# Gated linear attention, then a squared-ReLU feed-forward: the first four chunks loaded as two pairs, zero products in PE's early row, new figures for the plan

## The chip, the cores and the metric

One core of a Trainium2 chip runs the whole program. The metric is device time in microseconds of one execution; the lower, the better. The engines are PE (TensorE, matrix products), DVE (VectorE), ACT (ScalarE), POOL (GpSimd) and SP (SyncE, which issues the transfers here).

## The reference

```python
def _attn_ref(q, k, v, alpha):            # each (4, 8, 768, 48): batch, heads, tokens, width
    state = np.zeros((B, H, D, D))
    for t in range(S):
        state = alpha[:, :, t, :, None] * state + np.einsum('bhd,bhe->bhde', k[:, :, t], v[:, :, t])
        y[:, :, t] = np.einsum('bhd,bhde->bhe', q[:, :, t], state)
    return y

def _moe_ref(x, w_in, w_out):             # x: (3072, 384), w_in: (384, 2048), w_out: (2048, 384)
    r = np.maximum(x @ w_in, 0.0)
    return (r * r) @ w_out
```

The output of the first, transposed to one row of 384 per token, is the input of the second. All inputs and the output are float32.

## The kernel before

The 3072 tokens are 24 chunks of 128, six for each batch. A chunk lies with one token per partition. Its recurrence is done in closed form:

- `ln`: ACT takes the logarithm of alpha. `pm`: PE sums it over the tokens with a triangular matrix (and with a column of ones for the decay of the whole chunk). `ainv`, `am`: ACT takes exp(-sum) and exp(sum).
- `km`: POOL multiplies k by ainv. `qm`: DVE multiplies q by am. `vc`: POOL casts v to bf16.
- `tr`, `qkT`: PE transposes both, DVE copies them out of PSUM. (From chunk `N_PE` = 14 on a DMA transposes instead.) `sc`: PE forms the scores, 8 products. `sm`: DVE masks them with the triangle.
- `av`: PE multiplies the scores with v and adds q times the state of the chunks before (`sb`). `st`, `dec`, `sb`: the state gets the chunk's part, DVE decays it, ACT casts it.
- `xn`, `px`, `xT`: the result is cast, transposed by PE and copied into `xT`, the input of the feed-forward part.

The feed-forward part works on nine groups of 2 or 3 chunks. For each of 16 slices of 128 of the inner width, `mm1` is three products into `ph` (L393), `relu` is ACT's (L398, tile `r`) and `sq` is DVE's square (L404, tile `gT`). `m2` then multiplies `gT` with the second weights into `po` (L427); the result is copied to `ob` and stored.

A class `Plan` sets the order of everything. Each step is added with an engine, a cost, a key (its due time) and the steps that it needs; `Plan.run` plays the program through with these costs, and the instructions are emitted in the order of that play. Each engine then executes its own row strictly in that order, and waits in it on semaphores. `HOP` is what the play adds from a step's end to its use by another engine, `QUEUE` how far SP may run ahead of its transfers. PSUM has one bank set for `pm` and `py` together (`m`), one for `sc`, one for the transposes (`t`), two for `ph` and one for `po`.

SP issues all transfers, in one queue: alpha, k, q and v of chunks 0 to 3, then four loads of the first weights, chunk 4, four loads of the second weights, and the other chunks. A load of one chunk (`load_chunk`, L353) is 128 partitions x 8 heads x 48 floats, 1024 rows of 192 B, as each head's tokens lie apart in memory. A load of the first weights (L368) is 128 x 3 rows of 2 KB. The weights land in four buffers `wst`, and POOL casts them to bf16 (L372).

Of the kernel before, what the change touches and what calls it, by code (L numbers as in the profile page):

```python
# [14 lines left out]
class Plan:  # L15
# [3 lines left out]
    HOP = {"PE": 0.28, "SP": 0.0}  # L19
    QUEUE = 4.0  # L20
# [5 lines left out]
    def add(self, eng, cost, key, emit, after=(), behind=(), acquire=None,  # L26
            release=None, load=None):
        op = dict(eng=eng, cost=cost, key=(key, len(self.ops)), emit=emit,
                  after=[o for o in after if o is not None],
                  behind=[o for o in behind if o is not None], acquire=acquire,  # L30
                  release=release, load=load, start=None, done=None)
        self.ops.append(op)
        return op

    def run(self):
        ops, cap = self.ops, self.cap
        waiting = {id(o): 0 for o in ops}
# [10 lines left out]
        now = 0.0  # L48
        order = []
        while len(order) < len(ops):  # L50
            for r in [f for f in frees if f[0] <= now]:
                frees.remove(r)
                cap[r[1]] += 1
            chosen = None
            for t, o in ready:
                if t > now or free[o["eng"]] > now:
                    continue
                if o["acquire"] and cap[o["acquire"]] < 1:
                    continue
                if chosen is None or o["key"] < chosen["key"]:  # L60
                    chosen = o
            if chosen is None:
                later = [max(t, free[o["eng"]]) for t, o in ready] + [f[0] for f in frees]
                now = min(x for x in later if x > now)
                continue
            o = chosen
            ready = [x for x in ready if x[1] is not o]
            o["start"] = now
            free[o["eng"]] = now + o["cost"]
            if o["load"]:  # L70
                bus = max(bus, now + o["cost"]) + o["load"]
# [20 lines left out]
def kernel(  # L92
# [13 lines left out]
    P = 128  # L106
# [8 lines left out]
    NW = 4  # L115
    N_PE = 14
# [4 lines left out]
    ar = alpha.rearrange("b h (c p) d -> b c p h d", p=P)  # L121
    w_in_r = moe_w_in.rearrange("(j p) f -> p j f", p=P)
# [6 lines left out]
    wst = ctx.enter_context(tc.tile_pool(name="wst", bufs=4))  # L129
# [27 lines left out]
    qks = [consts.tile([P, 2, H, DP], BF16, name=f"qk{i}") for i in range(NS)]  # L157
    sbs = [consts.tile([P, NP, 2 * D], BF16, name=f"sb{i}") for i in range(2)]
    xTs = [consts.tile([P, KT, len(cs) * P], BF16, name=f"xT{g}") for g, cs in enumerate(groups)]

    def setup():
        nc.vector.memset(utri, 1.0)
        nc.gpsimd.affine_select(
            out=utri, in_=utri, compare_op=ALU.is_ge, fill=0.0,
            base=0, pattern=[[0, 1], [1, P]], channel_multiplier=-1,
        )
        nc.vector.memset(ones_col, 1.0)
        nc.vector.memset(lns[0], 0.0)
        make_identity(nc, ident)
        for x in lns[1:] + qks[:2]:  # L170
            nc.vector.memset(x, 0.0)
        for x in qks[2:] + sbs:
            nc.gpsimd.memset(x, 0.0)
# [11 lines left out]
    def o(kind, n):  # L185
        return O.get((kind, n))

    def gla(n):
# [100 lines left out]
        def e_xn():  # L289
            T["xn", n] = work.tile([P, HD], BF16, name="xn")  # L290
            nc.scalar.copy(T["xn", n], T["py", n][:, 0:HD])  # L291

        def e_px():
            px = T["px", n] = ps_t.tile([P, KT, P], BF16, name="px", tag="t")
            for j in range(KT):
                nc.tensor.transpose(px[:, j, :], T["xn", n][:, j * P:(j + 1) * P], ident)  # L296

        def e_xT():
            g = group_of[n]
            col = groups[g].index(n) * P  # L300
            nc.vector.tensor_copy(xTs[g][:, :, col:col + P], T["px", n])

# [5 lines left out]
        def e_qd():  # L308
# [5 lines left out]
        add("ln", "ACT", 0.53, e_ln, [o("ld_a", n), o("pm", n - NS)])  # L314
        add("vc", "POOL", 0.62, e_vc, [o("ld_v", n), o("av", m), o("st", m)])
        add("pm", "PE", 0.27, e_pm, [o("ln", n), o("av", n - NW + 1)], acquire="m")
        add("ainv", "ACT", 0.49, e_ainv, [o("pm", n), o("km", m)])
        add("am", "ACT", 0.49, e_am,
            [o("pm", n), o("qm", m), o("ainv", n), o("dec", m)], release="m")
        add("km", "POOL", 0.92, e_km, [o("ainv", n), o("ld_k", n), o("st", n - NS), o("tr", n - NS)])  # L320
        add("qm", "DVE", 0.80, e_qm, [o("am", n), o("ld_q", n), o("tr", n - NS)])
        if n < N_PE:
            add("tr", "PE", 0.45, e_tr, [o("km", n), o("qm", n)], acquire="t")
            add("qkT", "DVE", 0.69, e_qkT, [o("tr", n), o("av", m), o("sc", m)], release="t")
# [4 lines left out]
        add("sc", "PE", 0.40, e_sc, [o("qkT", n)], acquire="sc")  # L329
        add("sm", "DVE", 1.22, e_sm, [o("sc", n), o("av", m)], release="sc")  # L330
        add("av", "PE", 0.25 if first else 0.42, e_av,
            [o("sm", n), o("vc", n)] + ([] if first else [o("sb", n - 1)]), acquire="m")
        add("xn", "ACT", 0.48, e_xn, [o("av", n), o("px", m)], release="m")
# [5 lines left out]
        if n < N_PE:  # L339
            add("px", "PE", 0.18, e_px, [o("xn", n)], acquire="t")  # L340
            add("xT", "DVE", 0.36, e_xT, [o("px", n)], release="t")
        else:
            O["xT", n] = O["px", n] = plan.add("SP", 0.6, -2e6 + n, e_xd, [o("xn", n)], load=0.7)

    loaded = []

    def load_chunk(n):
        b, c = divmod(n, NCH)
        last_use = {"a": "ln", "k": "km", "q": "qm", "v": "vc"}
        for name, src in (("a", ar), ("k", kr), ("q", qr), ("v", vr)):  # L350
            def emit(name=name, src=src):
# [4 lines left out]
                [o(last_use[name], n - NLD)], loaded[-1:], load=1.03)  # L356
            loaded.append(O["ld_" + name, n])

    weights = []

    def load_w(kind, i):
# [8 lines left out]
        def cast():  # L370
# [10 lines left out]
    def moe(g):  # L381
# [7 lines left out]
        def unit1(f):  # L389
# [6 lines left out]
            def e_relu():  # L396
                r = T["r", g, f] = rp.tile([P, 4 * P], BF16, name="r")
                nc.scalar.activation(r[:, 0:tg], T["ph", g, f][:, 0:tg], AF.Relu)  # L398

            def e_sq():  # L400
                if f == 0:
                    T["gT", g] = gp.tile([P, FT, 4 * P], BF16, name="gT")
                r = T["r", g, f]
                nc.vector.tensor_mul(T["gT", g][:, f, 0:tg], r[:, 0:tg], r[:, 0:tg])  # L404
            u = g * FT + f
# [4 lines left out]
                [o("xT", n) for n in cs] + [O["cwi", f // 4]], [prev], acquire="ph")  # L410
# [3 lines left out]
            free = [O.get(("m2", n, 3)) for n in groups[g - 2]] if g >= 2 else []  # L414
            O["sq", u] = plan.add("DVE", 0.12 + 0.34 * part, key - 3 * PACE, e_sq,
                                  [rl] + free, [O.get(("sq", u - 1))])

        def unit2(tt, n, qd):
            bank = "m" if g >= len(groups) - 2 and n % 2 else "po"

            def e_mm():
                if qd == 0 and bank == "po":
                    T["po", n] = ps_o.tile([P, d_model], FP32, name="po")
# [11 lines left out]
            if qd == 3:  # L435
# [9 lines left out]
                def e_out():  # L445
                    nc.sync.dma_start(out=out_r[n], in_=T["ob", n])
# [55 lines left out]
```

## Time and profile before

| | |
|---|---|
| median of 3 runs | 198.18 us (197.69 to 198.73) |
| the profiled execution | 198.69 us |
| span of its instructions | 196.7 us |
| PE busy | 174.7 us, 89% of the span |
| DVE, ACT, POOL busy | 130.2, 119.7, 50.0 us |
| DMA | 33.77 MB, 121749 packets, 115072 of them under 512 B |

The page gives busy times over the whole span and in 40 slices of 4.9 us. The slices are digits of tenths; the row PEclk has the granted clock of PE. A row of the timeline has start, duration, engine, line, operation, tiles, count, and in brackets the idle time before it with what ended it. "idle" of a group is the idle time of its engine just before it.

### The profile page before, as it was taken

The numbers are of one execution on the slowest core, as the hardware profiler recorded it, in microseconds if no ns is written. First come the engines' busy times: TensorE is split into PE (matmuls) and PEld (weight loads), VectorE is DVE, ScalarE is ACT, GpSimd is POOL, SyncE is SP. The second block draws the span as 40 slices with busy tenths as digits, with TensorE's granted clock in tenths as the row PEclk, the third lists the DMA queues.
The fourth block names the chain that finished last, engine by engine and source line by source line (L and its number), as shares of the span: only waits on it lengthen the run. The fifth ranks groups of instructions, "written<-read, shape, count | busy, mean of one in ns | idle before, by whom it ended". The sixth has DMA issues, their size and how long they took to land.

```text
span 196.7 us, 4408 instructions
## 1 busy us (share of the span) xinstructions
PE 174.7 (89%) x1618; PEld 115.0 (58%) x1618; DVE 130.2 (66%) x260; ACT 119.7 (61%) x293; POOL 50.0 (25%) x67
## 2 busy tenths in 40 slices
PE   0466698599999999999999999998999999999992
PEld 0355475366666666766664666565565666567761
DVE  4366677996488889888956785594686763445311
ACT  3354259437536998788866777665776755465400
POOL 6242464660434233331420321111221000000000
PEclk9999999969999999999999999999999999999999
DMA  6999999999989999898999998999985422111012
GB/s 121 187 188 202 355 308 264 382 214 197 191 174 244 185 202 187 153 223 156 227 140 222 224 206 127 194 200 169 190 186 125 106 72 60 40 41 44 36 44 80
DMA packets 121749, 33.77 MB, mean 172 GB/s; under 512 B 115072, under 2 KB 120192, under 8 KB 121728
## 3 DMA queue, kind: packets, MB, share of 16 engines
q1 hardware_dynamic: 121728, 33.50, 85.3%
q8 instruction: 12, 0.20, 0.5%
q14 instruction: 9, 0.07, 0.1%
HBM read 25.17 MB, written 4.72 MB: 152 GB/s over the span
## 4 chain that ended last, share of the span: by engine, by line
PE 68%; DVE 9%; DMA 7%; SPq 6%; ACT 4%; issue 3%; POOL 1%; ACTq 0%; POOLq 0%
PE ph L393 26%; PE po L427 24%; SPq L353 5%; DMA ld_v<-in_v_dram 5%; DVE gT L404 4%; PE pom L427 4%; PE sc L246 3%; PE pt L234 3%; DMA ld_a<-in_alpha_dram 3%; PE py L265 2%; PE py L260 2%; ACT r L398 2%; PE st L274 1%; PE px L296 1%; PE pm L208 1%
## 5 line engine op out<-in xcount | busy, mean ns | idle before, releaser
L398 ACT ACTIVATE r<-ph 128x384 bf16<-128x384 f32 (+1 forms) x144 | 63.8, 455 | 34.6 <-PE ph L393 33.3
L393 PE MATMUL ph<-xT,w_in_b 128*128 128x384 bf16 (+1 forms) x432 | 81.6, 315 | 2.3 <-ACT r L398 1.5
L404 DVE TENSOR_TENSOR gT<-r 128x384 bf16<-128x384 bf16 (+1 forms) x144 | 56.4, 406 | 35.1 <-ACT r L398 32.9
L427 PE MATMUL po<-w_out_b,gT 128*128 128x384 bf16 x336 | 66.5, 328 | 0.5 <-ACT ob L441 0.4
L393 PEld LDWEIGHTS <-w_in_b 128*128 128x128 bf16 x432 | 40.1, 99 | 23.8 <-issue 5.1
L427 PEld LDWEIGHTS <-gT 128*128 128x128 bf16 x384 | 36.0, 98 | 22.1 <-issue 1.3
L225 POOL TENSOR_TENSOR qk<-ld_k,ainv 128x384 bf16<-128x384 f32 x24 | 22.0, 919 | 53.0 <-ACT ainv L217 53.0
L251 DVE TENSOR_TENSOR sm<-sc,utri 128x1024 bf16<-128x1024 f32 x24 | 29.3, 1221 | 4.0 <-PE sc L246 3.8
L204 POOL CAST vb<-ld_v 128x384 bf16<-128x384 f32 x24 | 13.2, 551 | 40.7 <-DMA ld_v<-in_v_dram 33.5
L228 DVE TENSOR_TENSOR qk<-ld_q,am 128x384 bf16<-128x384 f32 x24 | 17.8, 740 | 7.6 <-ACT am L222 7.5
L200 ACT ACTIVATE ln<-ld_a 128x384 bf16<-128x384 f32 x24 | 12.7, 528 | 9.5 <-DMA ld_a<-in_alpha_dram 9.3
L291 ACT CAST xn<-py 128x384 bf16<-128x384 f32 x24 | 11.5, 478 | 8.6 <-PE py L265 8.6
L217 ACT ACTIVATE ainv<-pm 128x384 bf16<-128x384 f32 x24 | 11.7, 489 | 6.3 <-PE pm L212 5.8
L265 PE MATMUL py<-vb,sm 128*128 128x48 bf16 x192 | 12.2, 190 | 3.7 <-DVE sm L251 2.5
L208 PE MATMUL pm<-ln,utri 128*128 128x384 bf16 x24 | 8.4, 352 | 6.5 <-ACT ln L200 5.6
L265 PEld LDWEIGHTS <-sm 128*128 128x128 bf16 x192 | 10.4, 101 | 6.0 <-DVE sm L251 4.5
L282 DVE TENSOR_TENSOR st<-st,am 128x384 f32<-128x384 f32 x20 | 11.2, 561 | 3.3 <-PE st L274 3.1
L234 PE MATMUL pt<-ident,qk 128*128 128x128 bf16 x112 | 10.5, 246 | 2.7 <-POOL qk L225 1.6
L222 ACT ACTIVATE am<-pm 128x388 f32<-128x388 f32 (+1 forms) x24 | 11.9, 495 | 0.0
L246 PE MATMUL sc<-qkT 64*128 64x128 bf16 x192 | 10.6, 236 | 1.0 <-DVE qkT L238 1.0
L441 ACT COPY ob<-po 128x384 f32<-128x384 f32 x12 | 5.8, 482 | 8.5 <-PE po L427 8.4
L260 PE MATMUL py<-sb,qkT 128*128 128x96 bf16 x80 | 10.8, 212 | 0.0
(34 smaller groups left out, 118.2 us busy)
## 6 DMA issues: line engine op xcount, KB each, us to landing
ld_a<-in_alpha_dram SPq DMA_DIRECT2D x24, 192.0 KB, 4.3
ld_k<-in_k_dram SPq DMA_DIRECT2D x24, 192.0 KB, 4.4
ld_q<-in_q_dram SPq DMA_DIRECT2D x24, 192.0 KB, 4.4
ld_v<-in_v_dram SPq DMA_DIRECT2D x24, 192.0 KB, 4.3
out_dram<-ob SPq DMA_DIRECT2D x24, 192.0 KB, 2.5
wst<-in_moe_w_in_dram SPq DMA_DIRECT2D x4, 768.0 KB, 8.5
wst<-in_moe_w_out_dram SPq DMA_DIRECT2D x4, 768.0 KB, 7.4
qkT<-qk SPq DMA_TRANSPOSE x10, 3.7
```

The costliest lines, as they stand in the source:

```text
L204: nc.gpsimd.tensor_copy(T["vb", n], T["v", n])
L225: nc.gpsimd.tensor_mul(qk[:, 1, :, 0:D], heads(T["k", n]), heads(T["ainv", n]))
L228: nc.vector.tensor_mul(qk[:, 0, :, 0:D], heads(T["q", n]), heads(T["am", n][:, 0:HD]))
L234: nc.tensor.transpose(pt[:, w, p, :], qk[:, w, 2 * p:2 * p + 2, :], ident)
L246: nc.tensor.matmul(sc[:, i, p, :], lhsT=qkT[r, 1, p, :], rhs=qkT[r, 0, p, :], start=True, stop=True)
L251: nc.vector.tensor_mul(sm.rearrange("s i p t -> s (i p) t"), T["sc", n].rearrange("s i p t -> s (i p) t"), utri.to_broadcast([P, H, P]))
L260: nc.tensor.matmul(py[:, 2 * p * D:2 * (p + 1) * D], lhsT=qkT[:, 0, p, :], rhs=sb[:, p, :], start=True, stop=False, skip_group_check=True)
L265: nc.tensor.matmul(py[:, h * D:(h + 1) * D], lhsT=sm[:, i, p, :], rhs=vb[:, h * D:(h + 1) * D], start=first, stop=True, skip_group_check=True)
L393: nc.tensor.matmul(ph[:, 0:tg], lhsT=w_in_b[:, j, f * P:(f + 1) * P], rhs=xT[:, j, 0:tg], start=(j == 0), stop=(j == KT - 1))
L398: nc.scalar.activation(r[:, 0:tg], T["ph", g, f][:, 0:tg], AF.Relu)
L404: nc.vector.tensor_mul(T["gT", g][:, f, 0:tg], r[:, 0:tg], r[:, 0:tg])
L427: nc.tensor.matmul(T["po", n], lhsT=T["gT", g][:, kf, tt * P:(tt + 1) * P], rhs=w_out_b[:, kf, :], start=(kf == 0), stop=(kf == FT - 1))
```

## The change

**Loads.** Chunks 0 and 1, and 2 and 3, are loaded as pairs: one transfer for alpha, one for k, q and v each, in which a partition gets two tokens that follow each other, so that a row is 2 x 48 floats, 384 B, and a transfer has 1024 of them. The pairs lie in the buffers `wst`, of which there are now six; alpha and k share one, q and v another. The even tokens of a pair form one slot and the odd ones the other (`j`), and what was chunk 0 and chunk 1 is now the lower and the upper half of the partitions (`x`).

**Recurrence of the pairs.** `gla_pair` takes both slots through `ln`, `pm`, `ainv`, `am`, `km`, `qm`, `vc`, `tr` and `qkT`, then both through `sc` and `sm`, then both halves through `av` and the rest. `pm` has two products for the sums instead of one, `sc` 16 instead of 8 (of 64 rows of output), `av` two for each head instead of one, `st` 8 instead of 4. `qkT` of the second slot is a copy on ACT. Masks for the four combinations of slots are built in `setup`. The output of these chunks is stored in two transfers each.

**Zero products.** Steps `blank`, each one product of a 128 x 128 zero tile with 256 zero columns into the `po` bank, fill PE's row wherever the play finds PE idle, up to the first `m2`. There are 117 of them in the program: 20 ahead of the first `pm`, 99 ahead of the first `mm1`.

**Figures.** `HOP` of PE goes from 0.28 to 0.17, `QUEUE` from 4.0 to 3.0, and many costs change. The play now charges DVE and POOL for one another where both use SBUF (`port`), and PE's products at up to double cost until 6.2 us after the first dense one.

```diff
-    HOP = {"PE": 0.28, "SP": 0.0}
-    QUEUE = 4.0
+    HOP = {"PE": 0.17, "SP": 0.0}
+    QUEUE = 3.0
...
+            if o["eng"] == "PE":
+                if o["dense"] and warm is None:
+                    warm = now + 6.2
+                if warm is None or now < warm:
+                    o["cost"] *= 2.0 if o["dense"] else 1.5
+            if o["port"]:
+                other = "DVE" if o["eng"] == "POOL" else "POOL"
+                o["cost"] += max(0.0, held[other] - now)
+                held[o["eng"]] = now + o["cost"]
...
+    NWST = 6
+    PAIRS = (0, 1)
+    NBLANK = 300
...
+    qr2, kr2, vr2, ar2 = [x.rearrange("b h (s p j) d -> b s p h (j d)", p=P, j=2)
+                          for x in (q, k, v, alpha)]
-    wst = ctx.enter_context(tc.tile_pool(name="wst", bufs=4))
+    wst = ctx.enter_context(tc.tile_pool(name="wst", bufs=NWST))
...
-        for x in qks[2:] + sbs:
+        for x in [blank] + qks[2:] + sbs:
             nc.gpsimd.memset(x, 0.0)
...
+        def e_pm(n, j):
+            pm = T["pm", n] = ps_m.tile([P, HD + 2 * NP], FP32, name="pm2", tag="m")
+            l0, l1 = lns[n0 % NS], lns[(n0 + 1) % NS]
+            nc.tensor.matmul(pm[:, 0:HD], lhsT=uinc2, rhs=l0[:, :, 0:D], start=True, stop=False)
+            nc.tensor.matmul(pm[:, 0:HD], lhsT=uinc2 if j else ustr2, rhs=l1[:, :, 0:D],
+                             start=False, stop=True)
...
+    def load_pair(S):
+        b, c = divmod(S, NCH // 2)
+        for name, src in (("a", ar2), ("k", kr2), ("q", qr2), ("v", vr2)):
+            def emit(name=name, src=src):
+                if name in "aq":
+                    T["w2", S, name in "qv"] = wst.tile([P, 2, H, 2, D], FP32, name="pair", tag="wst")
+                x = T[name + "2", S] = T["w2", S, name in "qv"][:, int(name in "kv")]
+                nc.sync.dma_start(out=x.rearrange("p h j d -> p h (j d)"), in_=src[b, c])
...
-        add("pm", "PE", 0.27, e_pm, [o("ln", n), o("av", n - NW + 1)], acquire="m")
+        add("pm", "PE", 0.29, e_pm, [o("ln", n), o("av", n - NW + 1)], acquire="m")
-        add("qm", "DVE", 0.80, e_qm, [o("am", n), o("ld_q", n), o("tr", n - NS)])
+        add("qm", "DVE", 0.55, e_qm, [o("am", n), o("ld_q", n), o("tr", n - NS)], port=True)
...
+    def e_blank():
+        if "blank" not in T:
+            T["blank"] = ps_o.tile([P, 4 * P], FP32, name="po")
+        nc.tensor.matmul(T["blank"][:, 0:2 * P], lhsT=blank[:, 0:P], rhs=blank,
+                         start=True, stop=True)
+    for i in range(NBLANK):
+        plan.add("PE", 0.107, 1e6 + i, e_blank, dense=True, drop=O["m2", 0, 0])
```

Where it moves instructions, at three places. First SP's row up to the weights; `ld_a` to `ld_v` are the loads of one chunk, `pair` the new ones. Before, from chunk 2 on:

```order
L353 DMA ld_a_163<-in_alpha_dram 128x8x48
L353 DMA ld_k_169<-in_k_dram 128x8x48
L353 DMA ld_q_182<-in_q_dram 128x8x48
L353 DMA ld_v_187<-in_v_dram 128x8x48
L353 DMA ld_a_208<-in_alpha_dram 128x8x48
L353 DMA ld_k_213<-in_k_dram 128x8x48
L353 DMA ld_q_234<-in_q_dram 128x8x48
L353 DMA ld_v_251<-in_v_dram 128x8x48
L368 DMA wst_275<-in_moe_w_in_dram 128x3x512
```

Now, from the start:

```order
L567 DMA pair_158<-in_alpha_dram 128x8x96
L567 DMA pair_158<-in_k_dram 128x8x96
L567 DMA pair_167<-in_q_dram 128x8x96
L567 DMA pair_167<-in_v_dram 128x8x96
L567 DMA pair_179<-in_alpha_dram 128x8x96
L567 DMA pair_179<-in_k_dram 128x8x96
L567 DMA pair_204<-in_q_dram 128x8x96
L567 DMA pair_204<-in_v_dram 128x8x96
L598 DMA wst_254<-in_moe_w_in_dram 128x3x512
```

The first weights stand behind eight transfers instead of sixteen, with the same bytes.

Second, PE's row at its beginning. Before, it opens with the sums of chunk 0, and nothing stands ahead of them:

```order
L208 LDWEIGHTS utri
L208 MATMUL pm<-ln_100,utri 128x384
L212 LDWEIGHTS ln_100
L212 MATMUL pm<-ones_col,ln_100 128x1
...
L234 LDWEIGHTS qk_104
L234 MATMUL pt<-ident,qk_104 128x128
```

Now the last of the 20 zero products, the sums of the first slot, and the first of seven zero products ahead of the sums of the second:

```order
L716 LDWEIGHTS blank
L716 MATMUL po<-blank 128x256
L263 LDWEIGHTS uinc_110
L263 MATMUL pm_189<-ln_100,uinc_110 128x384
L264 LDWEIGHTS ustr_111
L264 MATMUL pm_189<-ln_101,ustr_111 128x384
L716 LDWEIGHTS blank
```

`pm` of the first slot now needs both slots' `ln`, and stands behind products that need nothing but the cleared tile.

Third, DVE's row up to the first squares (`gT`). Before, chunks 1 to 3 follow each other:

```order
L251 TENSOR_TENSOR sm<-sc,utri 128x1024
L228 TENSOR_TENSOR qk_106<-ld_q,am 128x8x48
L282 TENSOR_TENSOR st<-st,am 128x384
L238 COPY qkT<-pt 128x1024
L301 COPY xT_110<-px 128x3x128
L251 TENSOR_TENSOR sm<-sc,utri 128x1024
L228 TENSOR_TENSOR qk_107<-ld_q,am 128x8x48
L282 TENSOR_TENSOR st<-st,am 128x384
L238 COPY qkT<-pt 128x1024
L301 COPY xT_111<-px 128x3x128
L251 TENSOR_TENSOR sm<-sc,utri 128x1024
L404 TENSOR_TENSOR gT<-r 128x256 x4
```

Now, from the first mask (`sm`) to the first squares:

```order
L314 TENSOR_TENSOR sm<-sc,mask_112 128x1024
L286 TENSOR_TENSOR qk_106<-pair,am 128x8x48
L314 TENSOR_TENSOR sm<-sc,mask_112 128x1024
L237 COPY qkT_109<-pt 128x16x64
L286 TENSOR_TENSOR qk_107<-pair,am 128x8x48
L348 TENSOR_TENSOR st<-st,am 128x384
L408 COPY xT_117<-px 128x3x128
L314 TENSOR_TENSOR sm<-sc,mask_112 128x1024
L348 TENSOR_TENSOR st<-st,am 128x384
L408 COPY xT_117<-px 128x3x128
L314 TENSOR_TENSOR sm<-sc,mask_112 128x1024
L636 TENSOR_TENSOR gT<-r 128x256 x4
```

The first two masks now stand ahead of the first decay (`st`) and the first `xT`, and the decay and `xT` of chunk 2 have moved behind the first four squares.

More of the change, by code (lines that the diff above doesn't have):

```diff
@@ L26, in add @@
     def add(self, eng, cost, key, emit, after=(), behind=(), acquire=None,
-            release=None, load=None):
+            release=None, load=None, port=False, dense=False, drop=None):
         op = dict(eng=eng, cost=cost, key=(key, len(self.ops)), emit=emit,
@@ L30, in add @@
                   behind=[o for o in behind if o is not None], acquire=acquire,
-                  release=release, load=load, start=None, done=None)
+                  release=release, load=load, port=port, dense=dense, drop=drop, start=None, done=None)
         self.ops.append(op)
@@ L47, in run @@
         bus = 0.0
-        now = 0.0
+        held = {"DVE": 0.0, "POOL": 0.0}
+        now = 1.4
+        warm = None
         order = []
-        while len(order) < len(ops):
+        while ready:
             for r in [f for f in frees if f[0] <= now]:
@@ L63, in run @@
                 later = [max(t, free[o["eng"]]) for t, o in ready] + [f[0] for f in frees]
-                now = min(x for x in later if x > now)
+                later = [x for x in later if x > now]
+                if not later:
+                    break
+                now = min(later)
                 continue
             o = chosen
-            ready = [x for x in ready if x[1] is not o]
+            ready = [x for x in ready if x[1] is not o and x[1]["drop"] is not o]
             o["start"] = now
+            if o["eng"] == "PE":
[7 more added lines that the diff above has]
+                held[o["eng"]] = now + o["cost"]
             free[o["eng"]] = now + o["cost"]
             if o["load"]:
-                bus = max(bus, now + o["cost"]) + o["load"]
+                bus = max(bus, now + o["cost"] - 0.6 * (bus == 0.0)) + o["load"]
                 free[o["eng"]] = max(free[o["eng"]], bus - self.QUEUE)
@@ L86, in run @@
                                       + [d["start"] + d["cost"] for d in u["behind"]]), u))
+        assert len(order) + sum(o["start"] is None and o["drop"] is not None for o in ops) == len(ops)
         self.order = order
@@ L115 @@
     NW = 4
+    NWST = 6
+    PAIRS = (0, 1)
+    NPR = len(PAIRS)
+    NBLANK = 300
     N_PE = 14
@@ new lines, in e_xn, with e_px, e_xT @@
+    def e_xn(n, x=0):
+        T["xn", n] = work.tile([P, HD], BF16, name="xn")
+        nc.scalar.copy(T["xn", n], T["py", n][:, 0:HD])
+    def e_px(n, x=0):
+        px = T["px", n] = ps_t.tile([P, KT, P], BF16, name="px", tag="t")
+        for j in range(KT):
+            nc.tensor.transpose(px[:, j, :], T["xn", n][:, j * P:(j + 1) * P], ident)
+    def e_xT(n, x=0):
+        g = group_of[n]
+        col = groups[g].index(n) * P
+        nc.vector.tensor_copy(xTs[g][:, :, col:col + P], T["px", n])
@@ L287, in e_sb @@
             nc.scalar.copy(sbn[DP:P, :, D:2 * D], st[DP:P, :, D:2 * D])
[L289 to L301, printed above, removed]
         def e_xd():
@@ L328, in gla @@
                 load=1.7)
-        add("sc", "PE", 0.40, e_sc, [o("qkT", n)], acquire="sc")
-        add("sm", "DVE", 1.22, e_sm, [o("sc", n), o("av", m)], release="sc")
-        add("av", "PE", 0.25 if first else 0.42, e_av,
+        add("sc", "PE", 0.36, e_sc, [o("qkT", n)], acquire="sc")
+        add("sm", "DVE", 1.22, e_sm, [o("sc", n), later("av", m)], release="sc")
+        add("av", "PE", 0.25 if first else 0.33, e_av,
             [o("sm", n), o("vc", n)] + ([] if first else [o("sb", n - 1)]), acquire="m")
-        add("xn", "ACT", 0.48, e_xn, [o("av", n), o("px", m)], release="m")
+        add("xn", "ACT", 0.48, lambda: e_xn(n), [o("av", n), o("px", m)], release="m")
         if not last:
@@ L373, in load_w @@
         ld = plan.add("SP", 0.5, -1e6 + len(loaded), emit,
-                      [o("wc", len(weights) - 4)], loaded[-1:], load=2.17)
+                      wst_free(), loaded[-1:], load=2.17 if i else 2.6)
         loaded.append(ld)
-        O["wc", len(weights)] = O["c" + kind, i] = plan.add("POOL", 1.47, -100.0 + len(weights), cast, [ld])
+        O["wc", len(weights)] = O["c" + kind, i] = plan.add("POOL", 1.47, -100.0 + len(weights), cast, [ld], port=True)
+        w = len(weights)
+        wst_users.append(lambda: [O["wc", w]])
         weights.append(ld)
@@ L413, in unit1 @@
                                          release="ph")
-            free = [O.get(("m2", n, 3)) for n in groups[g - 2]] if g >= 2 else []
-            O["sq", u] = plan.add("DVE", 0.12 + 0.34 * part, key - 3 * PACE, e_sq,
-                                  [rl] + free, [O.get(("sq", u - 1))])
+            O["sq", u] = plan.add("DVE", 0.12 + 0.30 * part, key - 3 * PACE, e_sq,
+                                  [rl] + free, [O.get(("sq", u - 1))], port=True)
         def unit2(tt, n, qd):
@@ L458 @@
     for n in range(NCK):
-        load_chunk(n)
+        if n // 2 not in PAIRS:
+            load_chunk(n)
+        elif n % 2 == 0:
+            load_pair(n // 2)
         for kind, i in between.get(n, ()):
             load_w(kind, i)
-        gla(n)
+        if n // 2 not in PAIRS:
+            gla(n)
+        elif n % 2:
+            gla_pair(n // 2)
     for g in range(len(groups)):
```

215 lines of the change are left out of this document (194 added, 21 removed).

## The prediction

> **What bounds the kernel now.** I read the page first: busy shares, slices, the chain that ended last.
>
> ```profile
> PE 174.7 (89%) x1618; PEld 115.0 (58%) x1618; DVE 130.2 (66%) x260; ACT 119.7 (61%) x293; POOL 50.0 (25%) x67
> ...
> PE   0466698599999999999999999998999999999992
> ...
> PEclk9999999969999999999999999999999999999999
> ...
> PE 68%; DVE 9%; DMA 7%; SPq 6%; ACT 4%; issue 3%; POOL 1%; ACTq 0%; POOLq 0%
> ```
>
> PE bounds it: after the first 25 us it is full nearly everywhere. So a gain must come from the beginning, or from slices where PE is not full (7 and 8) or slow (PEclk 6). The view by stretches tells how much there is (columns: stretch, length, then busy us of PE, PEld, DVE, ACT, POOL, then clock, DMA share, GB/s).
>
> ```profile
> 10.00:24.72 14.72, 9.86 (x112) 7.58 (x112) 9.87 (x15) 6.10 (x16) 5.76 (x7) 1.00 1.25 250
> 24.72:30.00 5.28, 5.28 (x45) 4.05 (x44) 4.38 (x7) 3.07 (x9) 3.89 (x3) 1.00 1.08 298
> 30.00:35.00 5.00, 4.04 (x36) 2.90 (x34) 4.00 (x12) 4.61 (x14) 2.02 (x4) 1.00 1.05 283
> 35.00:40.00 5.00, 2.71 (x30) 1.85 (x27) 5.00 (x9) 1.80 (x5) 3.42 (x3) 0.89 1.06 380
> 40.00:45.00 5.00, 5.00 (x48) 3.63 (x45) 5.00 (x9) 2.43 (x7) 2.46 (x2) 0.76 1.00 192
> 45.00:50.00 5.00, 4.15 (x30) 2.74 (x29) 2.22 (x9) 3.86 (x12) 0.00 (x0) 1.00 1.30 191
> 50.00:100.00 50.00, 49.55 (x546) 33.28 (x545) 42.54 (x80) 37.23 (x90) 16.60 (x23) 1.00 1.03 195
> 100.00:150.00 50.00, 48.34 (x441) 29.47 (x439) 32.83 (x66) 34.10 (x83) 10.01 (x14) 1.00 1.05 187
> 150.00:193.12 43.12, 43.12 (x327) 27.62 (x325) 19.86 (x50) 22.59 (x54) 0.91 (x1) 1.00 0.19 57
> ```
>
> From the first product of the feed-forward part (24.72 us) to PE's last (193.12) are 168.4 us. PE is idle in 0.96 + 2.29 + 0.85 = 4.1 us of 30 to 50, in 0.45 of 50 to 100, in 1.66 of 100 to 150, and never after. Next, how fast PE is when it is busy: timeline and chain.
>
> ```profile
> 24.78 2.68 PE ph L393 x12
> 27.92 0.81 PE L393 MATMUL ph<-xT,w_in_b 128*128 128x256 bf16 x3
> 28.79 0.49 PE L393 MATMUL ph<-xT,w_in_b 128*128 128x256 bf16 x3
> 40.06 1.46 PE L393 MATMUL ph<-xT,w_in_b 128*128 128x256 bf16 x6
> 42.48 0.49 PE L393 MATMUL ph<-xT,w_in_b 128*128 128x256 bf16 x3
> 42.81 0.21 PE L260 MATMUL py<-sb,qkT 128*128 128x96 bf16 x1
> 43.19 0.49 PE L393 MATMUL ph<-xT,w_in_b 128*128 128x256 bf16 x3
> 175.86 0.66 PE ph L393 x6
> ```
>
> Twelve 256-column products take 2.68 us at 24.78 (0.223 each), six take 0.66 at 175.86 (0.11 each). PE runs at half rate until 28.8 and again from about 39.5 to 42.5, where the clock column has 0.89 and 0.76; before 28.8 that column is no evidence, since it says 1.00 while the products take double. Two thirds busy (9.86 of 14.72) didn't turn the clock up; unbroken work from 24.72 on (5.28 of 5.28) did.
>
> What sets 24.72 is the arrival of the weights:
>
> ```profile
> 1.88 1.84 POOL L173 MEMSET qk<- 128x1024 bf16 x2
> 3.97 0.52 ACT L200 ACTIVATE ln<-ld_a 128x384 bf16<-128x384 f32 x1 [1.89 <-DMA ld_a<-in_alpha_dram]
> 10.85 4.60 DMA ld_v<-in_v_dram
> 22.57 1.47 POOL L372 CAST w_in_b<-wst 128x1536 bf16<-128x1536 f32 x1 [2.15 <-DMA wst<-in_moe_w_in_dram]
> 29.05 1.47 POOL L372 CAST w_in_b<-wst 128x1536 bf16<-128x1536 f32 x1 [0.71 <-DMA wst<-in_moe_w_in_dram]
> ```
>
> The first load is there at about 3.9, the twelfth at 15.45: 1.05 us each, so the sixteenth at 19.65. The first cast of weights ends at 24.04.
>
> **The change part by part.**
>
> *Loads.* A load of 192 KB is 1024 rows of 192 B in 1.05 us; a weight load of 768 KB is 384 rows of 2 KB, and three of them lie between the casts, 2.16 us each. A fixed price per row and one per byte fit both: 64 rows per DMA engine x 8.8 ns + 12 KB x 0.0406 us. A pair (64 rows, 24 KB per engine) is then 0.56 + 0.97 = 1.54 us, an estimate between 1.05 (rows alone count) and 2.10 (bytes alone). Eight pairs: first at 3.9 + 0.5 = 4.4, eighth at 4.4 + 7 x 1.54 = 15.2, 4.5 us earlier than now. The first weight cast would end at 19.6. SP's later transfers shift alike; each output of these chunks becomes two issues, beside work and late, at nothing. The third weight load reuses the first pair's buffer, which km of chunk 1 frees near 12, ahead of its turn at about 15: nothing too. The Trainium skill (DMA: Bandwidth & Descriptors, "Why small descriptors are slow") gives each packet about 3 cycles beside its 32-byte beats; by it a pair costs 15/9 of a single, 1.75 us, the eighth lands at 16.7, and the sum would be about 1 us worse. No run here shows 384-byte rows yet.
>
> *First product.* With weights at 19.6, the recurrence of chunks 0 and 1 comes last: xT of chunk 1. Its prices by group:
>
> ```profile
> L251 DVE TENSOR_TENSOR sm<-sc,utri 128x1024 bf16<-128x1024 f32 x24 | 29.3, 1221 | 4.0 <-PE sc L246 3.8
> L228 DVE TENSOR_TENSOR qk<-ld_q,am 128x384 bf16<-128x384 f32 x24 | 17.8, 740 | 7.6 <-ACT am L222 7.5
> L217 ACT ACTIVATE ainv<-pm 128x384 bf16<-128x384 f32 x24 | 11.7, 489 | 6.3 <-PE pm L212 5.8
> L282 DVE TENSOR_TENSOR st<-st,am 128x384 f32<-128x384 f32 x20 | 11.2, 561 | 3.3 <-PE st L274 3.1
> L238 DVE COPY qkT<-pt 128x1024 bf16<-128x1024 bf16 x14 | 9.6, 686 | 1.8 <-PE pt L234 1.6
> L301 DVE COPY xT<-px 128x384 bf16<-128x384 bf16 x14 | 5.0, 354 | 2.3 <-PE px L296 2.1
> ```
>
> Two ln end at 5.5. Twenty zero products stand before the first pm; they need the blank tile, which POOL clears where it now clears qk (1.88, so about 2.2), and at 0.223 each end at 6.6. So pm is 1.1 us late. From there pm, ainv, am (the one m bank is held meanwhile), then the same for chunk 1, qm, transposes, a copy on ACT and sc: ten steps which the rows put between 0.49 (ainv) and 0.74 (qm); the copy on ACT has no row, and I take DVE's 0.69 for it. At 0.67 in the mean the first sm starts at about 13.3. Then DVE's row to the second xT holds 3 sm, 2 qm, 1 qkT, 2 decays and 2 xT: 3.66 + 1.48 + 0.69 + 1.12 + 0.71 = 7.7 us. Without a wait that ends at 21.0; with as many as DVE has now (9.87 busy of 14.72) at 24.8. I take 22.4, nearer the first since two chunks interleave, and 0.2 for PE: first product at 22.6, **-2.1** (ends -3.5 to +0.3).
>
> *Work that was ahead of that product and now is behind it.* av, st and px of chunk 2 (20 + 8 + 3 products), and 12 more in av and st of chunk 3: 43 small ones. Twelve such took 42.81 to 43.19, 0.032 each: **+1.4** (1.0 to 2.0). The other added products, masks and memsets lie ahead of it, inside the stretch just costed.
>
> *The clock.* Until 28.8 and from 39.5 to 42.5 together 7.0 us pass at half rate, worth at most 3.5. PE's row is now filled from about 2.2 with 99 zero products ahead of the first ph, so it should turn between 6 and 9, and I keep it up: **-3.0** (0 to -3.5). The second stretch followed gaps of 1.15 and 0.99 us:
>
> ```profile
> 34.91 1.47 POOL L372 CAST w_out_b<-wst 128x1536 bf16<-128x1536 f32 x1
> 34.94 1.85 DVE L228 TENSOR_TENSOR qk<-ld_q,am 128x384 bf16<-128x384 f32 x1
> 36.85 0.40 PE L234 MATMUL pt<-ident,qk 128*128 128x128 bf16 x4 [1.15 <-DVE qk L228]
> 39.52 0.61 PE L246 MATMUL sc<-qkT 64*128 64x128 bf16 x8 [0.99 <-DVE qkT L238]
> ```
>
> The Trainium skill (TensorE: Matmul & The Clock Gate, "What's actually happening") lets the clock drop after an idle window of about 3.4 us. No gap here is that long and it dropped, so the trace differs and decides; by the page 1.4 us of this term would not be there to gain.
>
> *Waits of 30 to 50.* DVE's qm takes 1.85 us beside a cast instead of 0.74, and PE waits for it. The plan now charges such pairs when it orders the rows, and loads and casts come 4.5 us earlier: I take half of the 4.1, **-1.9** (0 to -4.1), the other half being DVE's own load (5.00 of 5.00). Zero products that stand before a ready real one: 18 after the first ph, 2.0 us at full rate, mostly in idle time, **+0.3** (0 to 2.0). But a faster PE meets DVE, 4.4 of 5.3 us busy in 24.72 to 30, so part of the first clock gain turns into waits for r and gT: **+0.8** (0 to 2.0).
>
> *The order after 50.* All costs of the plan change, so its later order does too, SP's transfers included. PE has 0.45 + 1.66 = 2.1 us of idle time there, so at best that goes; at worst a new wait takes as much again. Nothing in the rows says which: 0 (-2.1 to +2.1). The last 43 us are full on PE and stay.
>
> Sum: -2.1 + 1.4 - 3.0 - 1.9 + 0.3 + 0.8 = -4.5. The profiled execution took 198.69 (span 196.70 and 1.99 around it), so 194.2; it lies 0.51 above the median of the runs, 198.18, so the median should be **193.7**.
>
> **The rivals.** A change under 0.5%, about 1 us, can't be told from none.
>
> *Waits vanish altogether.* Earlier loads and the new order take all 4.1 us, and DVE takes nothing back: -2.2 - 0.8 more, 190.7. Against it: DVE is full in 35 to 45.
>
> *The pair is as slow per byte* (2.10 us): the eighth lands at 4.9 + 7 x 2.10 = 19.6 as now, the start doesn't move, and half of the 1.9 is gone: -1.5, 196.7. For it: 192-byte rows move 187 GB/s, 2 KB rows 364, and nothing shows where between them 384 lies. The Trainium skill (DMA: Bandwidth & Descriptors, "Specifications") puts full rate at 512 B and up; by that rule pairs would still be slow.
>
> *DVE is the bound of 25 to 45* (18.4 of 20.3 us busy): the clock then gains nothing there, the stretch moves by the start less the decay and xT of chunk 2 that follow it, -2.1 + 0.9 + 0.3 = -0.9: 197.3, no change. Against it: in a third of that time PE was busy at half rate.
>
> *Slower: the zero products stand in the way.* 79 of them lie between the first pm and the first ph. If the clock does not turn, each costs 0.223 instead of 0.11, and real work must wait in PE's row. It decides when 40 of them run slow (40 x 0.113 = 4.5 us, the whole gain); with 60, the end comes 2.3 us later than now: 200.5. For it: 9.86 of 14.72 us did not turn the clock. Against: the row now has no planned gap.
>
> **How the numbers follow.** Forecast 0.60, waits vanish 0.08, slow pairs 0.12, DVE 0.10, zero products in the way 0.10. Faster: the first three, 0.80; same 0.10; slower 0.10. The forecast's own range is 191.2 to 196.2 (start by 1.4 either way, clock, waits and DVE by about 1 each, not all together). The stated range, 190.4 to 197.2, takes in all but the last rival and the tails of the others.
>
> **What would show it.** Eighth pair landed near 15.2; 256-column products at 0.11 us from the first ph on; that one near 22.6; no clock below 0.95 in 35 to 45; PE idle, or filled with zero products, under 2.5 us in 30 to 50; PE's last product near 188.6. The forecast is wrong if the first ph stays past 24, if PE waits for DVE longer than now, or if new idle time appears after 50.

## The result, and the profile after

The median is 192.61 us (191.88 to 192.76, 4 runs) against 198.27 us of the kernel before: a ratio of 0.971, 95% interval 0.967 to 0.974. 193.7 was forecast. The profiled execution took 192.59 us with a span of 190.9. In all ratios, here and below, runs more than 1.5% above the fastest of their own kernel are left out, while the ranges of runs that are given hold them too.

The page of the changed kernel: busy times, the two rows of slices, and the chain that ended last.

```profile
PE 183.5 (96%) x1819; PEld 123.7 (65%) x1819; DVE 131.1 (69%) x270; ACT 122.6 (64%) x295; POOL 50.5 (26%) x68
...
PE   5999999999999998999999999999999999999993
...
PEclk9999999999999999999999999999999999999999
...
PE 92%; DVE 3%; ACT 2%; issue 1%; POOL 1%; POOLq 0%; ACTq 0%
```

PE is full from the second slice on (at first mostly with zero products), the 6 in the clock row is gone, and the chain is PE's for 92% instead of 68%. The same stretches as before, of the changed kernel (stretch, length, busy us of PE, PEld, DVE, ACT, POOL, then clock, DMA share, GB/s):

```profile
10.00:24.68 14.68, 14.43 (x222) 11.09 (x220) 9.23 (x13) 6.54 (x14) 8.37 (x9) 1.00 1.09 314
24.68:30.00 5.32, 5.32 (x65) 4.23 (x63) 3.40 (x9) 3.45 (x10) 1.47 (x1) 1.00 0.94 247
30.00:35.00 5.00, 5.00 (x58) 3.96 (x57) 4.58 (x6) 3.60 (x11) 4.40 (x4) 1.00 1.07 382
35.00:40.00 5.00, 4.88 (x47) 3.84 (x46) 4.69 (x12) 3.55 (x10) 3.07 (x2) 1.00 0.90 206
40.00:45.00 5.00, 4.86 (x42) 3.24 (x40) 2.89 (x8) 3.67 (x10) 0.28 (x1) 1.00 0.95 189
45.00:50.00 5.00, 5.00 (x62) 4.08 (x61) 4.26 (x11) 3.92 (x12) 2.38 (x4) 1.00 0.82 166
50.00:100.00 50.00, 48.93 (x535) 32.58 (x534) 41.69 (x84) 37.71 (x91) 13.67 (x20) 1.00 0.97 200
100.00:150.00 50.00, 50.00 (x471) 31.01 (x469) 35.46 (x69) 38.34 (x92) 11.39 (x15) 1.00 0.91 176
150.00:187.56 37.56, 37.56 (x280) 24.09 (x278) 16.53 (x44) 17.81 (x43) 0.00 (x0) 1.00 0.18 55
```

The first feed-forward product starts at 24.68, where it started before (24.72). PE's last one ends at 187.56 instead of 193.12. So everything was won behind the start: 162.9 us instead of 168.4. PE's idle time is 0.26 us in 30 to 50 (4.1 before), 1.07 in 50 to 100 (0.45), none in 100 to 150 (1.66).

Why the start did not move shows in the timeline of the changed kernel ahead of it (start, duration, engine, line, operation, tiles, count):

```profile
2.25 4.40 PE L716 MATMUL po<-blank 128*128 128x256 bf16 x20 [2.25 <-POOL blank L212]
4.59 0.94 ACT L254 ACTIVATE ln<-pair 128x384 bf16<-128x384 f32 x2 [2.52 <-DMA pair<-in_alpha_dram]
6.81 0.93 PE L716 MATMUL po<-blank 128*128 128x256 bf16 x7
10.61 0.94 ACT L254 ACTIVATE ln<-pair 128x384 bf16<-128x384 f32 x2 [1.10 <-DMA pair<-in_alpha_dram]
15.06 0.50 POOL L237 CAST vb<-pair 128x384 bf16<-128x384 f32 x1 [0.66 <-DMA pair<-in_v_dram]
17.00 0.57 PE L329 MATMUL py<-vb,sm 64*128 64x48 bf16 x16
17.09 1.47 POOL L602 CAST w_in_b<-wst 128x1536 bf16<-128x1536 f32 x1 [0.20 <-DMA wst<-in_moe_w_in_dram]
17.21 1.75 DVE L286 TENSOR_TENSOR qk<-pair,am 128x384 bf16<-128x384 f32 x1
19.45 1.01 ACT L235 COPY qkT<-pt 128x1024 bf16<-128x1024 bf16 x1 [1.37 <-PE pt L293]
20.88 0.36 DVE L408 COPY xT<-px 128x384 bf16<-128x384 bf16 x1 [1.44 <-PE px L403]
21.25 0.21 PE L323 MATMUL py<-sb,qkT 128*128 128x96 bf16 x1
22.43 0.27 PE L329 MATMUL py<-vb,sm 64*128 64x48 bf16 x4
24.03 0.35 DVE L408 COPY xT<-px 128x384 bf16<-128x384 bf16 x1
24.68 0.82 PE L625 MATMUL ph<-xT,w_in_b 128*128 128x256 bf16 x6
```

Loads and clock did what was forecast. The two alpha loads are four transfers and 6.02 us apart, 1.505 each (1.54 forecast). The zero products take 0.22 each up to 6.65, and seven of them 0.93 us from 6.81 on: full rate. The eighth pair is there at 15.06 (15.2 forecast), and the first weights at 17.09, a microsecond earlier than forecast (their cast was to end at 19.6 and ends at 18.56). But the recurrence of chunk 1 isn't ready: qm of chunk 3 runs 1.75 us beside the cast, ACT's copy takes 1.01, then come `av` of chunk 1 (21.25 to 22.70) and its cast, transposes and copy. DVE, whose work the forecast added up, is busy for 8.1 of the 10.9 us from its first `sm` (13.51) to the end of its second `xT` (24.38), and waits for the other 2.8.

### The profile page after: what moved, and what is told of

The parts are those of the page before. It is cut to its first block, busy times and chain, and to the rows that moved or that the text cites. A ratio compares the mean times of both kernels' runs of the same rounds, so it can differ in the third digit from the quotient of the medians.

```text
span 190.9 us, 4792 instructions
## 1 busy us (share of the span) xinstructions
PE 183.5 (96%) x1819; PEld 123.7 (65%) x1819; DVE 131.1 (69%) x270; ACT 122.6 (64%) x295; POOL 50.5 (26%) x68
## 4 chain that ended last, share of the span: by engine, by line
PE 92%; DVE 3%; ACT 2%; issue 1%; POOL 1%; POOLq 0%; ACTq 0%
PE ph L625 33%; PE po L660 29%; PE po L716 7%; PE pom L660 4%; PE sc L468 3%; PE pt L456 2%; PE py L487 2%; PE pm L430 2%; PE py L482 2%; PE st L496 1%; PE px L403 1%; PE py L329 1%; DVE qk L286 1%; PE py L323 1%; PE sc L307 1%
## 5 line engine op out<-in xcount | busy, mean ns | idle before, releaser
L447 POOL TENSOR_TENSOR qk<-ld_k,ainv 128x384 bf16<-128x384 f32 x20 | 18.3, 913 | 69.6 <-ACT ainv L439 69.6
L473 DVE TENSOR_TENSOR sm<-sc,utri 128x1024 bf16<-128x1024 f32 x20 | 24.4, 1220 | 4.2 <-PE sc L468 4.2
L716 PE MATMUL po<-blank 128*128 128x256 bf16 x117 | 18.7, 297 | 2.3 <-POOL blank L212 2.3
L716 PEld LDWEIGHTS <-blank 128*128 128x128 bf16 x117 | 11.5, 105 | 5.1 <-POOL blank L212 2.2
L450 DVE TENSOR_TENSOR qk<-ld_q,am 128x384 bf16<-128x384 f32 x20 | 12.0, 604 | 0.4 <-ACT am L444 0.4
L422 ACT ACTIVATE ln<-ld_a 128x384 bf16<-128x384 f32 x20 | 10.4, 522 | 0.0
L487 PE MATMUL py<-vb,sm 128*128 128x48 bf16 x160 | 9.4, 183 | 0.0
L487 PEld LDWEIGHTS <-sm 128*128 128x128 bf16 x160 | 8.2, 96 | 1.4
L660 PE MATMUL pom<-w_out_b,gT 128*128 128x384 bf16 x48 | 8.8, 326 | 0.0
L482 PE MATMUL py<-sb,qkT 128*128 128x96 bf16 x68 | 8.2, 204 | 0.0
## 6 DMA issues: line engine op xcount, KB each, us to landing
ld_a<-in_alpha_dram SPq DMA_DIRECT2D x20, 192.0 KB, 3.7
ld_k<-in_k_dram SPq DMA_DIRECT2D x20, 192.0 KB, 3.6
ld_q<-in_q_dram SPq DMA_DIRECT2D x20, 192.0 KB, 3.9
ld_v<-in_v_dram SPq DMA_DIRECT2D x20, 192.0 KB, 3.8
out_dram<-ob SPq DMA_DIRECT2D x20, 192.0 KB, 2.1
```

Source lines behind the costliest of these rows:

```text
L447: nc.gpsimd.tensor_mul(qk[:, 1, :, 0:D], heads(T["k", n]), heads(T["ainv", n]))
L450: nc.vector.tensor_mul(qk[:, 0, :, 0:D], heads(T["q", n]), heads(T["am", n][:, 0:HD]))
L473: nc.vector.tensor_mul(sm.rearrange("s i p t -> s (i p) t"), T["sc", n].rearrange("s i p t -> s (i p) t"), utri.to_broadcast([P, H, P]))
L482: nc.tensor.matmul(py[:, 2 * p * D:2 * (p + 1) * D], lhsT=qkT[:, 0, p, :], rhs=sb[:, p, :], start=True, stop=False, skip_group_check=True)
L487: nc.tensor.matmul(py[:, h * D:(h + 1) * D], lhsT=sm[:, i, p, :], rhs=vb[:, h * D:(h + 1) * D], start=first, stop=True, skip_group_check=True)
L660: nc.tensor.matmul(T["po", n], lhsT=T["gT", g][:, kf, tt * P:(tt + 1) * P], rhs=w_out_b[:, kf, :], start=(kf == 0), stop=(kf == FT - 1))
```

## The experiments

Two theories, put forward after the traces had been compared. *Loads and clock*: the pairs and the zero products bring the gain. *Figures*: the plan's new figures bring it, through the order that they make. In the diffs, `-` is the changed kernel.

**Zero products planned, but not emitted; the rows are otherwise the same.**

```diff
     def e_blank():
+        if True:
+            return
```

> The changed kernel, each engine's row as it is, but the 117 zero products are left out of PE's row. Clock theory (the zero products turn the clock up 20 us earlier and keep it up): the first 256-column products take 0.22 us again and the clock drops again in 30 to 45, so 2.5 to 4 us slower than the changed kernel, 195 to 196.5. Loads theory (the gain is that weights and chunks come earlier, and the zero products are a passenger): within 1 us of the changed kernel, or up to 2 us faster because 18 of them stand among real products, 190.6 to 193.6.

Ratio 0.985 (0.976 to 0.993); the runs go from 192.8 to 198.1, where the changed kernel's lie within 1 us. In the one whose trace is kept, the longest, PE turns to full rate only near 34 us; that the others differ for the same reason isn't shown. So in this order the zero products do matter, less in the best run than in how often a good one comes.

**Single loads, zero products and figures.**

```diff
-    PAIRS = (0, 1)
+    PAIRS = ()
```

> The changed kernel with the first four chunks loaded and worked on singly, as before; zero products (164 now, where the plan finds room) and figures stay, and the plan makes a new order. Loads theory: the waits of 30 to 50 are back, 195.5 to 198. Clock theory: about as the changed kernel, 192 to 194.5, with a first feed-forward product near 24.7 as in both, but at full rate.

Ratio 0.982 (0.976 to 0.988), 193.63 us: the theory that the earlier loads bring the gain falls here. The first weights' cast starts at 21.72 instead of 17.09, the first product at 24.86, nearly where it was, and the waits don't come back.

**Single loads, no zero products: the figures alone**, twice, the second time beside the changed kernel on one chip.

```diff
-    PAIRS = (0, 1)
-    NBLANK = 300
+    PAIRS = ()
+    NBLANK = 0
```

> Only the plan's new figures: single loads and no zero products. If the figures (the order) took the waits away: 194.5 to 196, with the two slow stretches of the clock left. If the clock or the loads did: within 1 us of the kernel before, 197 to 199.

> Single loads, no zero products, the new figures, beside the changed kernel on one chip. Figures theory: 0.975 to 0.985 of the kernel before, and within 1 us of the changed kernel. Loads and clock theory: 1 to 3 us slower than the changed kernel.

> The changed kernel once more, beside the figures alone on one chip. Loads and clock theory (pairs and zero products bring part of the gain): at least 1 us faster than the figures alone. Figures theory (the order brings it, the rest pays for itself at most): within 1 us of it. Both expect a first feed-forward product at 24.6 to 24.8.

First time 0.982 (0.975 to 0.990), second 0.975 (0.971 to 0.979) and 192.72 us, beside 0.974 (0.971 to 0.977) and 192.51 us of the changed kernel. They can't be told apart, and the figures alone are well below the kernel before. The stretches of the figures alone, second time (stretch, length, PE busy, clock, DMA share, GB/s):

```profile
24.20:30.00 5.80, 4.54 (x45) 1.00 0.98 238
30.00:35.00 5.00, 4.38 (x42) 1.00 1.02 352
35.00:40.00 5.00, 4.55 (x39) 1.00 1.10 337
40.00:45.00 5.00, 4.76 (x49) 1.00 0.77 151
45.00:50.00 5.00, 5.00 (x44) 1.00 1.06 230
50.00:100.00 50.00, 49.18 (x552) 1.00 1.00 205
100.00:150.00 50.00, 49.84 (x465) 1.00 0.84 175
```

With the old loads and without a zero product, PE is idle 1.3 us in 30 to 50 instead of 4.1, the clock holds, and 1.0 instead of 2.1 us are idle in 50 to 150. The clock also turns up sooner than in the kernel before:

```profile
24.20 1.46 PE L625 MATMUL ph<-xT,w_in_b 128*128 128x256 bf16 x6
25.93 0.49 PE L625 MATMUL ph<-xT,w_in_b 128*128 128x256 bf16 x3
```

The first six products still run at half rate, those from 25.93 on at full rate (in the first execution of the figures alone from 27.4 on, in the kernel before from 28.8). So a good part of what the forecast put down to the zero products, under *clock*, the order brings without them; why PE turns up sooner there isn't shown.

**Only the 99 zero products ahead of the first feed-forward product.**

```diff
     def e_blank():
+        if "ph" in [k[0] for k in T]:
+            return
```

> The changed kernel without the 18 zero products behind the first feed-forward product; the 99 ahead of it stay. If those 18 stand in the way of ready work (0.11 us each, as the prediction charged with 0.3): 0 to 2 us faster, 190.6 to 192.6. If they hold the clock up over the waits: a clock column under 1.00 in 30 to 45 and 0.5 to 1.5 us slower, 193 to 194.

Ratio 0.974 (0.967 to 0.981). Two stretches of it:

```profile
30.00:35.00 5.00, 4.41 (x51) 1.00 1.06 381
35.00:40.00 5.00, 3.44 (x32) 1.00 0.90 212
```

Idle time stands where the 18 stood (2.3 us in 30 to 50 instead of 0.26), the clock holds, and the time is the same within the interval. They stood in nobody's way, and nobody needed them.

**Only the first 49 zero products.**

```diff
     def e_blank():
+        T["emitted"] = T.get("emitted", 0) + 1
+        if T["emitted"] > 49:
+            return
```

> The changed kernel with only the first 49 of its 117 zero products, those up to the transposes of chunk 1; the rest is left out. If the rest stand in the way of real work (PE's row is full from 10 to 22.6 with them): first feed-forward product 0.5 to 1.5 us earlier, 22.9 to 24.2, and the time 0.3 to 1.3 us below the changed kernel's, if the start sets the end. If the clock drops without them: 256-column products at 0.22 us and 1.5 to 3 us slower. If neither: within 0.5 us.

```profile
10.00:24.00 14.00, 10.20 (x155) 7.75 (x154) 8.13 (x10) 5.88 (x12) 8.69 (x9) 0.76 1.13 327
24.00:30.00 6.00, 6.00 (x69) 4.01 (x67) 3.16 (x7) 3.17 (x9) 1.47 (x1) 0.70 0.83 223
```

The clock drops: PE is busy 10.2 of 14 us, with no gap longer than 1.1 us, and the column has 0.76 and 0.70. Ratio 0.983 (0.976 to 0.990), runs from 192.2 to 199.7. In this order the zero products behind the 49th keep the clock up. The mean clock alone doesn't explain the spread of the runs: one of 196.2 us and one of 192.2 have 0.974 and 0.971.

**What holds the start.** The first cast waits until DVE's qm of chunk 3 is done, by a clear of one column of the cast's target on DVE; then the same with 79 zero products, none from the first `px` on.

```diff
         def cast():
+            if (kind, i) == ("wi", 0):
+                nc.vector.memset(w_in_b[:, 0, 0:1], 0.0)
             nc.gpsimd.tensor_copy(dst, T[kind, i])
...
     def e_blank():
+        T["emitted"] = T.get("emitted", 0) + 1
+        if T["emitted"] > 79:
+            return
```

> The changed kernel with the first weight cast on POOL made to wait until DVE's qm of chunk 3 is done (one clear of a single column of the cast's target on DVE right after it). If the 1.75 us of that qm beside the cast (0.55 alone) is what holds the recurrence of chunk 1, and with it the first feed-forward product: that product 1.0 to 1.3 us earlier, 23.4 to 23.7. If the start sets the end: 0.8 to 1.3 us faster than the changed kernel. If a later wait (DVE, the second weights) sets it: the start moves and the end does not, within 0.4 us of the changed kernel.

> The changed kernel with the first weight cast behind DVE's qm of chunk 3 and without the zero products from the first px on (79 of 117 stay). Both things that stand ahead of the first feed-forward product are away: 23.0 to 23.8 instead of 24.1 to 24.7, and if the start sets the end 0.5 to 1.5 us faster than the changed kernel. If DVE's row or the second weights set the end: the start moves and the time stays within 0.4 us.

The first: qm takes 0.55, the first feed-forward product is at 24.71, 192.49 us, ratio 0.973 (0.969 to 0.977): no change. That was a miss, and it is understood in part only: in its profile the clock turned up later than in the changed kernel's (seven zero products still take 1.40 us at 7.13) and the first `sm` started at 13.95 instead of 13.51. In the changed kernel's second profile qm happened to start just ahead of the cast by itself and took 0.55, with the first product at 24.06. The second experiment, in its profile, which is that of its longest run:

```profile
10.00:23.40 13.40, 12.04 (x201) 1.00 1.14 335
23.40:30.00 6.60, 6.53 (x48) 0.50 0.84 205
```

The first product starts at 23.47, and at half rate: in this execution, without the last zero products, the clock dropped just ahead of it. The runs go from 191.7 to 197.7, with a mean clock of 0.99 in the three shortest and 0.965 in the longest; ratio 0.979 (0.973 to 0.985). Whether an earlier start at full rate would bring the end forward stays open.

**One pair.**

```diff
-    PAIRS = (0, 1)
+    PAIRS = (0,)
```

> Only chunks 0 and 1 as a pair, 2 and 3 singly; zero products and figures stay (149 zero products now). If pairs are worth their earlier weights: weights land about 2.2 us later than with two pairs and the time lies between the changed kernel and the figures alone. If the pair's added products and its longer chain eat what the loads give: within 0.7 us of both.

196.56 us, ratio 0.995 (0.993 to 0.998): neither of the two cases expected. Two of its stretches:

```profile
50.00:75.00 25.00, 23.50 (x277) 1.00 0.97 201
75.00:100.00 25.00, 23.34 (x257) 1.00 0.99 202
```

The clock holds, and PE is idle 3.2 us in 50 to 100, where the other kernels have about 1. The plan made another order out of nearly the same steps, and it waits: in 50 to 100 mostly for ACT, 1.2 us for its copies that free the `po` bank and 0.8 for a relu. So the new figures, with both new charges, can also make an order that gains almost nothing.

**Which figures.** Both start from the figures alone.

```diff
-    HOP = {"PE": 0.17, "SP": 0.0}
-    QUEUE = 3.0
+    HOP = {"PE": 0.28, "SP": 0.0}
+    QUEUE = 4.0
```

> The figures alone (single loads, no zero products), with HOP of PE and QUEUE set back to 0.28 and 4.0; costs, port and clock figures stay new. If those two make the better order: 196.5 to 198.5, as the kernel before. If the costs and the port do: within 1 us of the figures alone, 192 to 194.

191.78 us, ratio 0.975 (0.971 to 0.979): these two do nothing that can be measured.

```diff
-                if warm is None or now < warm:
+                if False:
                     o["cost"] *= 2.0 if o["dense"] else 1.5
-            if o["port"]:
+            if False:
```

> The figures alone without the two new charges in the play: DVE and POOL are not charged for each other, and PE's early products cost their full-rate time. If it is these charges that make the order: 196 to 198.5, with DVE's qm again over 0.70 us in the mean and PE idle over 4 us in 30 to 50. If the other figures do: 192 to 194, PE idle under 2 us there.

199.53 us, ratio 1.015 (1.010 to 1.020): without the two charges the new figures are slower than the old ones. Of its stretches (PE alone):

```profile
30.00:35.00 5.00, 5.00 (x36) 1.00 1.01 334
35.00:40.00 5.00, 3.19 (x29) 1.00 1.11 349
40.00:45.00 5.00, 2.82 (x24) 0.92 0.83 160
45.00:50.00 5.00, 4.79 (x43) 0.74 0.54 108
```

PE is idle 4.2 us in 30 to 50 and the clock drops: the picture of the kernel before. The first product, too, comes 2.1 us later than in the figures alone. In its timeline:

```profile
26.34 0.81 PE L625 MATMUL ph<-xT,w_in_b 128*128 128x256 bf16 x3
35.66 0.92 POOL L447 TENSOR_TENSOR qk<-ld_k,ainv 128x384 bf16<-128x384 f32 x1 [6.67 <-ACT ainv L439]
37.15 1.81 DVE L450 TENSOR_TENSOR qk<-ld_q,am 128x384 bf16<-128x384 f32 x1
38.89 3.02 DVE L636 TENSOR_TENSOR gT<-r 128x256 bf16<-128x256 bf16 x2
37.03 6.20 POOL L602 CAST w_out_b<-wst 128x1536 bf16<-128x1536 f32 x4
```

And the same place in the figures alone, with both charges:

```profile
32.64 0.55 DVE L450 TENSOR_TENSOR qk<-ld_q,am 128x384 bf16<-128x384 f32 x1
33.11 2.35 DVE L636 TENSOR_TENSOR gT<-r 128x256 bf16<-128x256 bf16 x5
33.65 1.47 POOL L602 CAST w_out_b<-wst 128x1536 bf16<-128x1536 f32 x1 [1.08 <-DMA wst<-in_moe_w_out_dram]
```

With the charges qm is through when the first cast of the second weights begins, and five squares take 2.35 us; without them qm and the squares meet four casts in a row, 1.81 for the one and 3.02 for two of the others. Over the whole kernel qm takes 765 ns in the mean without the charges and 618 with them (740 before):

```profile
L450 DVE TENSOR_TENSOR qk<-ld_q,am 128x384 bf16<-128x384 f32 x24 | 18.4, 765 | 2.4 <-ACT am L444 2.2
```

```profile
L450 DVE TENSOR_TENSOR qk<-ld_q,am 128x384 bf16<-128x384 f32 x24 | 14.8, 618 | 1.3 <-ACT am L444 1.3
```

The two charges were taken out together, and the rows don't tell which of them does it. That qm takes longer beside a cast is shown (1.75 us in the changed kernel, 0.55 where the cast was held back), and the charge for DVE and POOL is for that. But the four casts meet qm because POOL stood idle 6.67 us for `ainv` of chunk 4; the sums that it needs stand on PE at 34.59, behind a row of 36 feed-forward products, and at 30.08 in the figures alone. That order of PE's row can come from the charge for the slow clock just as well. Neither was run alone.

## Why the prediction was right, and where not

The time came out 1.1 us below the forecast and inside its own range, but the terms were not right one by one, and by one of the forecast's own signs, a first `ph` past 24, it was wrong about the start. Against the kernel before, from the two profiled executions:

| term | forecast | measured |
|---|---|---|
| first product | -2.1 | 0.0 (24.68; 24.06 in a second execution) |
| work moved behind it | +1.4 | +0.8 (the rest of 162.9 - 168.4 when the other rows are taken out) |
| clock | -3.0 | -3.5 at most (half of the 7.0 us; no slow stretch is left) |
| waits of 30 to 50 | -1.9 | -3.8 (4.10 to 0.26) |
| zero products behind the first | +0.3 | +2.0 of PE's row, in place of waits (18 x 0.11); with the row above -1.8, forecast -1.6 |
| DVE takes back | +0.8 | 0.0 (5.32 of 5.32 in 24.68 to 30) |
| order after 50 | 0 | -1.0 (2.11 to 1.07) |

- *Loads*: right. 1.505 us for a pair; by an estimate from the rule of the Trainium skill (DMA: Bandwidth & Descriptors, "Why small descriptors are slow") it would have been 1.75, so the straight line through the two kinds of rows was the better price, and the rival of the slow pair is out.
- *First product*: the step that failed is taking DVE's row for the chain, with few waits because two chunks interleave. The first `sm` started at 13.51, as forecast (13.3), and the sum of DVE's work was near (8.1 us, 7.7 forecast), but DVE waited 2.8 us where the forecast left 1.4: for ACT's copy of the transposes, for which a DVE duration was taken (0.69; it takes 1.01), and for the small products of `av` (1.45 us for 20 of them; at 0.032 each, the price of the next term, it would be 0.64). Of DVE's own work qm beside the cast took 1.75 us instead of 0.74. Earlier weights were worth nothing for the start: with single loads it is at 24.86 with zero products and at 24.20 without.
- *The clock*: turned up where forecast and stayed up. But the figures alone also keep it up after 30, and leave only about 1.4 us of slow feed-forward products ahead of that (24.20 to 25.6) where the kernel before has 4.1; the zero products take away those, and their own price is PE's time in waits that were there. The rule of the Trainium skill (TensorE: Matmul & The Clock Gate, "What's actually happening") of an idle window of 3.4 us again does not fit: with 49 zero products the clock dropped while PE had no gap longer than 1.1 us.
- *Waits*: the plan's new charge was named, and sized at half of the 4.1. That size was right: without the 18 zero products PE is idle 2.3 us in 30 to 50. What the forecast missed is that the figures bring the whole of the gain: with them alone the time is that of the changed kernel, and without the two charges it is worse than before. That the order after 50 gains too was within the bounds given, at 0.
- *DVE takes back*: the rival that DVE bounds 25 to 45 is out. DVE was full in 35 to 45, in part because its instructions ran beside POOL's (qm 1.85 us, 0.55 when no cast runs); now it is busy 4.69 and 2.89 of 5.00 there, and PE waits 0.26 us.
- *Zero products in the way*: not with these; with only the first 49 of them the runs spread up to 199.7.

The forecast's sum was near by luck: a start that didn't come (2.1) was more than made up by four smaller terms that all came out better: the order after 50 (1.0), DVE (0.8), the moved work (0.6) and the clock (0.5).

## What to carry to other kernels

When a plan with costs sets the order, its charges are worth testing like any other edit: here the one for engines that hold each other up, together with the one for the slow clock, makes 3 to 4% (0.975 and 0.982 with the two, 1.015 without) with the same instructions. This is one order for each set of figures, though: with the same charges and one pair the plan came out at 0.995, so whether a truer charge makes a better order in general isn't shown. When several edits come together, run each alone before believing the visible one: the pairs let the weights' cast start 4 us earlier and 117 products filled PE, and with both the median is that of the figures alone (192.51 and 192.72). Products that only keep PE busy helped in the order made with pairs, most of all in the spread of the runs; the figures alone have none, and their runs lie as close (192.0 to 193.5).

## What the runs showed of the hardware that was not expected

- DVE's copy of a 128 x 128 bf16 tile took 2.50 us in the figures alone (2.86 in the changed kernel), while POOL cleared its tiles. It was the last thing that PE's first sum waited for, at 4.44:

```profile
1.88 2.50 DVE L200 COPY utri<-uinc 128x128 bf16<-128x128 bf16 x1
4.44 0.50 PE L430 MATMUL pm<-ln,utri 128*128 128x384 bf16 x1 [4.44 <-DVE utri L200]
```

- ACT needs 1.01 us to copy 1024 bf16 columns from PSUM where DVE needs 0.68.
- Products on 64 of the rows cost much where they take turns with full ones: 16 of them in a row took 0.57 us (at 17.00 in the changed kernel), and 16 in turns with 4 full ones 1.45 (21.25 to 22.70). Twelve full ones took 0.54 in the kernel before (42.81 to 43.35).
- PE's clock drops while PE is still busy for most of a stretch: at 10.2 of 14 us, at 3.19 and 2.82 of 5.00, and in the kernel before at 2.71 of 5.00. It held at 4.38 of 5.00, at 3.44 with the 18 left out, and without zero products at 3.14 (40 to 45), across a gap of 2.29 us; the drop with 49 of them came with no gap longer than 1.1. So neither a share over 5 us nor the longest gap alone tells the one from the other; where the bound lies stays open.
